# First units' PV held in SBUF, idle identity products early, later softmax sums by head and turned by DMA, and ranks of the plan found by a search

## The chip, the cores and the metric

One core of one Trainium2 chip. The metric is the device time of one execution in microseconds (us), median of several runs. The profile's "span" (first to last instruction) is 1.5 to 2 us shorter. TensorE, VectorE (DVE), ScalarE (ACT), GpSimd (POOL) and the sync engine (SP) run their own instruction streams, each strictly in the order in which the program was emitted; they meet at semaphores. SP here does nothing but issue DMAs.

## The reference, cut to what matters

```python
# q, k, v: 4 batches x 8 heads x 768 positions x 64, float32
scores = (q @ k.T) / 8                     # per batch and head
# heads 0, 2, 6 ("retrieval"): causal; the other five: causal and (first 4 keys or the last 64 keys)
a = exp(scores - max) / (sum + 1e-9)
attn = a @ v                               # -> x: 3072 tokens x 512
h = x @ w_in                               # 512 x 2048
g = h / (1 + exp(-beta * h))
out = g @ w_out                            # 2048 x 512, float32
```

## The kernel before

The work is cut into eight units of 384 queries (`n` = 2·batch + half). A unit's attention makes transposed q and k, scores, exp (no maximum is subtracted), masks, the sums of each softmax row, their reciprocals spread over 64 rows per head (`R`), `PV`, and `xT = PV * R`. Then come 16 up-projection steps (4 products of 384 columns each; ScalarE takes a tanh, VectorE finishes the gate) and 48 down-projection products of 512 columns. Units 0 and 1 start the kernel; the attention of every later unit is laid between the projections of the units before it.

Nobody writes that order down. Every operation is added to a plan with a rank (`key`), an engine, a cost in us, what it needs and gives, and the buffers that it takes and drops. The plan simulates all engines and a DMA bus, takes at each step the operation that can start first (lowest rank on a tie), and the program is then emitted in the simulated order.

```python
    def run(self):
        # ... choose the operation (t, e, o) that can start earliest, lowest rank first ...
            if dma:
                bus = max(bus, t + 0.5) + dma
                end = bus + 1.9            # when the transfer is taken to have landed
        # ...
        return [(f, e) for _, _, f, e in sorted(order, key=lambda x: x[:2])]
```

Once emitted, the order is fixed. If a step takes longer on the chip than the plan thought, everything behind it on its engine waits.

The reciprocals go two ways. Units 0 to 3 (`RD = 4`) split them into two bf16 parts and spread them with four products; units 4 to 7 write them to DRAM and read them back with broadcast. Units 0 to 3 (`TD = 4`) transpose q and k on TensorE, the others by DMA.

```python
    def sums(x):          # 128-column products; columns of queries j*128.. land on rows 32*j + head
        # ... pe.matmul(sm[32*j:32*j+32, 0:128], l, e, ...): 35 of them (even units) or 63 (odd)

    def recips_d(x):                                   # VectorE, straight from PSUM
        x.rec = rp.tile([96, 128], F32, name="rec")
        dve.reciprocal(x.rec, x.sm[0:96, 0:128])

    def spread_w(x):                                   # three DMAs to DRAM
        x.rd = dp.tile([8, TU, 128], F32, name="rd")
        for j in range(TU):
            sp.dma_start(out=x.rd[:, j, :], in_=x.rec[32 * j:32 * j + 8, :])
    # spread_r: two DMAs read rd with broadcast into R (128 x 4 x 384)

    # in the plan, units n >= RD:
            add(key["S"] + 0.1, "dve", 1.0, lambda: recips_d(x), needs=[("sum", n)], gives=[("rec", n)], ...)
            add(key["S"] + 0.2, "sp", 1.4, lambda: spread_w(x), needs=[("rec", n)], gives=[("rd", n)], dma=0.1, ...)
            add(key["S"] + 0.3, "sp", 0.9, lambda: spread_r(x), needs=[("rd", n)], gives=[...R...], dma=4.0, ...)
```

The softmax here doesn't subtract the row's maximum and nothing guards it: scores larger than these inputs give would overflow.

Of the kernel before, what the change touches and what calls it, by code (L numbers as in the profile page):

```python
# [24 lines left out]
TD = 4  # L25
RD = 4
# [23 lines left out]
class _Plan:  # L50
# [16 lines left out]
    def run(self):  # L67
# [11 lines left out]
        while any(left.values()):  # L79
# [39 lines left out]
            now[e] = end  # L119
# [16 lines left out]
            order.append((t, i, f, e))  # L136
            self.log.append((t, i, t + cost, e, key, gives))
        return [(f, e) for _, _, f, e in sorted(order, key=lambda x: x[:2])]
# [3 lines left out]
def kernel(  # L142
# [23 lines left out]
    def tpool(name, bufs, space=None):  # L166
# [4 lines left out]
        q2f=5, k2f=5, vf=3, wf=3, c=4, vb=2, vs=2, xT=2, gT=2, t=2, osb=3, R=1, rec=1, hl=1, VK=2,  # L171
# [56 lines left out]
    def const_ident():  # L228
        pool.memset(warm, 0.0)
        pool.memset(identf, 1.0)  # L230
        aff(identf, 1, -1, 0, 128)
        aff(identf, -1, 1, 0, 128)
        act.activation(out=warm, in_=warm, func=AF.Exp)
        dve.tensor_copy(out=ident, in_=identf)
# [127 lines left out]
    def sink_rows(b):  # L362

        t = bank((2 * b, "k"))
        pe.matmul(t[0:96, :], sink_sel, v_b[b][:, 0, :, :].rearrange("p h d -> p (h d)"), start=True, stop=True)
        held["sinks"] = t
# [32 lines left out]
    def load_beta():  # L399
        held["beta"] = rp.tile([96, 128], F32, name="rec")[0:FO]  # L400
        act.dma_start(out=held["beta"], in_=moe_beta.rearrange("(fo fi) -> fo fi", fi=128))
# [11 lines left out]

    def transposes(x, pi):
        t = ps.tile([128, 2, 512], BF16, name=f"b{plan.where['b', (x.n, 'T', pi)]}")
        x.ps[pi] = t[:, :, 0:NQ].rearrange("p a (t n) -> p a t n", t=TU)
        c = x.ld.pop((pi, "c"))
        for i in range(2):
            for t in range(TU):
                pe.transpose(x.ps[pi][:, i, t, :], c[:, i, t * 128:(t + 1) * 128], ident)  # L420

    def qk_copy(x, pi, eng, i0=0, n=2):
        dst = x.QK[:, i0:i0 + n, pi, x.u * NQ:(x.u + 1) * NQ].rearrange("d a (p t) -> d a p t", t=TU)
        cast(eng, dst, x.ps[pi][:, i0:i0 + n].rearrange("d a t p -> d a p t"))
# [33 lines left out]
    def scores(x, pi, ri):  # L458
# [6 lines left out]
        ps = banks((x.n, pi, ri))  # L465
        halves = rounds[ri]
# [78 lines left out]
    def sums(x):  # L545
        sm = bank((x.n, "s"))
        byj = [[] for _ in range(TU)]
# [17 lines left out]

    def recips_d(x):
        x.rec = rp.tile([96, 128], F32, name="rec")
        dve.reciprocal(x.rec, x.sm[0:96, 0:128])

    def spread_w(x):  # L570
        x.rd = dp.tile([8, TU, 128], F32, name="rd")
        for j in range(TU):
            sp.dma_start(out=x.rd[:, j, :], in_=x.rec[32 * j:32 * j + 8, :])
# [21 lines left out]
    def spread(x, t):  # L595
        if t == 0:
            x.R = rp.tile([128, NP, NQ], F32, name="R", bufs=RINGS["R"])
# [5 lines left out]
    def spread_copy(x, t, eng):  # L603
        cast(eng, x.R[:, t, :], x.ps.pop(("R", t))[:, 0:NQ])

    def pv(x, g):
        vb = v_b[x.b]
        o = banks((x.n, "v", g))
        ops = [[], []]
# [78 lines left out]
    def attention(n, key, early):  # L688
        x = units[n]
        b, u = x.b, x.u  # L690
        gate = ([("begun", "o", NS // 2 - 1)] if b else []) + ([("h", n - 2, 0)] if n > 3 else [])

        for pi in range(NP if n < TD else 0):
            for nm in ("q2", "k2"):
                e = "act" if n == 0 and nm == "k2" else "sp"
                add(key["lq"] + 0.01 * pi, e, 0.47, lambda pi=pi, nm=nm, e=e: load_qk(x, pi, nm, ENG[e]), dma=0.64, needs=gate,
                    gives=[("f", n, pi, nm)], take=[(nm + "f", (n, pi), 1)])
                e = [("pool", "dve"), ("pool", "act")][n] if early else ("pool",)
                add(key["T"][pi] - 2 + (0.001 if nm == "k2" else 0), e, [{"dve": 0.3, "pool": 0.47, "act": 0.41}[i] for i in e],
# [3 lines left out]
                    take=[("c", (n, pi), 1)] if nm == "q2" else [], drop=[(nm + "f", (n, pi))])  # L703
        if n >= TD:
            for i in range(2):
                add(key["lq"] + 0.1 * i, "sp", 3.0, lambda i=i: load_block(x, i), dma=3.9, needs=gate,
                    gives=[("f", n, i)], take=[("wf", (n, "b", i), TU)])
                for j in range(TU):
                    add(key["T"][0] - 2 + 0.5 * j + 0.1 * i, "pool", 0.7, lambda i=i, j=j: cast_block(x, i, j, pool),
                        needs=[("f", n, i)] + ([("c", n, 0, j)] if i else []), gives=[("c", n, i, j)],  # L710
                        take=[("c", (n, j), 1)] if i == 0 else [], drop=[("wf", (n, "b", i))])
            for j in range(TU):
                add(key["T"][0] + 0.5 * j, "sp", 1.25, lambda j=j: turn_block(x, j), dma=0.7,
                    needs=[("c", n, 0, j), ("c", n, 1, j)] + [("sc", n - 4 + v, pi) for pi in range(NP) for v in range(2 - u) if n >= 4],
                    gives=[("QKb", n, j)], drop=[("c", (n, j))])
            add(key["T"][0] + 1.5, "pool", 0.02, lambda: None, needs=[("QKb", n, j) for j in range(TU)],
                gives=[("QK", n, pi, i) for pi in range(NP) for i in range(2)])
        for j in range(TU):
# [6 lines left out]
            add(key["cv"] + 0.5 * j, "pool", 0.58, lambda j=j: cast_v(x, j, pool),  # L725
                needs=[("vf", n, j)] + ([("v", n - u, 0)] if (u, j) != (0, 0) else []),
                gives=[("v", n, j)], drop=[("wf" if b else "vf", (n, 0 if b else j))], take=[("vb", b, 5)] if (u, j) == (0, 0) else [])
        add(key["cv"] + 2, ("dve", "pool") if n else ("pool",), (1.2, 3.0), lambda e: shift_v(x, ENG[e]), port=True,
            needs=[("v", n, j) for j in range(TU)] + ([("v", n - 1, TU - 1)] if u else []), gives=[("vs", n)], take=[("vs", n, 2)])
        if not u:  # L730
            add(key["cv"] + 3, "pe", 0.23, lambda: sink_rows(b), needs=[("v", n, 0), ("const", "sink")], gives=[("VKp", b)],
                take=[("b", (n, "k"), 1)], drop=[("vb", b)])
            add(key["cv"] + 3.1, "dve", 0.6, lambda: sink_copy(b), needs=[("VKp", b)], gives=[("VK", b)],
                take=[("VK", b, 4)], drop=[("b", (n, "k"))])
# [4 lines left out]
        for pi in range(NP if n < TD else 0):  # L739
            k0 = key["T"][pi]  # L740
            wait = [("sc", n - 4 + j, pi) for j in range(2 - u) if n >= 4]
            add(k0, "pe", 0.34 if early else 0.2, lambda pi=pi: transposes(x, pi), needs=[("c", n, pi, "q2"), ("c", n, pi, "k2"), ("const", "ident")],
                gives=[("T", n, pi)], take=[("b", (n, "T", pi), 2 if early else 1)], drop=[("c", (n, pi))])
            if early:
                for i in range(2):
                    add(k0 + 0.1, ("act", "dve"), (0.37, 0.465), lambda e, pi=pi, i=i: qk_copy(x, pi, ENG[e], i, 1),
                        needs=[("T", n, pi)] + wait, gives=[("QK", n, pi, i)], drop=[("b", (n, "T", pi))])
            else:
                add(k0 + 0.1, ("act", "dve"), (0.7, 0.87), lambda e, pi=pi: qk_copy(x, pi, ENG[e]),
                    needs=[("T", n, pi)] + wait, gives=[("QK", n, pi, 0), ("QK", n, pi, 1)], drop=[("b", (n, "T", pi))])  # L750
        for pi in range(1, NP):
            if not u:
                k0 = key["T"][pi]
                add(k0 + 0.2, ("pool", "dve"), (0.35, 0.3), lambda e, pi=pi: ks_copy(x, pi, ENG[e]), port=True,
# [5 lines left out]
        for bi, bu in enumerate(bursts):  # L760
            k0 = key["B"][bi] if not early else key["T"][bu[0][0]] + 0.5 + 0.2 * bu[0][1]
# [18 lines left out]
            for j, (pi, ri) in enumerate(bu):  # L780
                half = rounds_of(pi, u)[ri][1] is None
                add(k0 + 0.1 + 0.02 * j, "act", 0.38 if half else 0.7, lambda pi=pi, ri=ri: exps(x, pi, ri),
                    needs=[("S", n, pi, ri)], gives=[("E", n, pi, ri)], drop=[("sp", (n, pi, ri))])
                c = mask_cost(pi, ri, u)
                if c:
                    add(k0 + 0.2 + 0.02 * j, "dve", c, lambda pi=pi, ri=ri: masks(x, pi, ri, dve), port=True,
# [3 lines left out]
        add(key["S"], "pe", [0.85, 1.35][u], lambda: sums(x), needs=M + [("const", "esel"), ("const", "sink")], gives=[("sum", n)],  # L790
            take=[("b", (n, "s"), 1)], drop=[(f"es{pi}_{u}", n) for pi in range(NP)], mode="sum")
        if n < RD:
            add(key["S"] + 0.1, "dve", 0.88, lambda: recips(x), needs=[("sum", n)], gives=[("rec", n)])
            add(key["S"] + 0.2, "dve", 1.3, lambda: split(x), needs=[("rec", n), ("const", "sel"), ("const", "zero")], gives=[("hl", n)],
                take=[("hl", n, NP)], drop=[("b", (n, "s"))])
            for t in range(NP):
                add(key["S"] + 0.3 + 0.01 * t, "pe", 0.18, lambda t=t: spread(x, t),
                    needs=[("hl", n)] + ([("sb", n, 0)] if t else []), gives=[("sb", n, t)],
                    take=[("b", (n, "R", t), 1)] + ([("R", n, 2)] if t == 0 else []), drop=[("hl", n)])
                add(key["S"] + 0.4, ("act", "dve"), (0.37, 0.465), lambda e, t=t: spread_copy(x, t, ENG[e]),  # L800
                    needs=[("sb", n, t)], gives=[("R", n, t)], drop=[("b", (n, "R", t))])
        else:
            add(key["S"] + 0.1, "dve", 1.0, lambda: recips_d(x), needs=[("sum", n)], gives=[("rec", n)],
                take=[("rec", n, 1)], drop=[("b", (n, "s"))])
            add(key["S"] + 0.2, "sp", 1.4, lambda: spread_w(x), needs=[("rec", n)], gives=[("rd", n)], dma=0.1, drop=[("rec", n)])
            add(key["S"] + 0.3, "sp", 0.9, lambda: spread_r(x), needs=[("rd", n)], gives=[("R", n, t) for t in range(NP)], dma=4.0,
                take=[("R", n, 2)])
        for g in range(2):
            drop = [(f"es{pi}_{u}", n) for pi in [(0, 1, 3), (2, 3)][g]] + [("vb", b), ("vs", n), ("VK", b)]
            add(key["PV"][g], "pe", [[0.5, 0.67], [1.05, 1.2]][u][g], lambda g=g: pv(x, g),  # L810
                needs=M + vready + [("rec", n) if n < RD else ("R", n, 0)], gives=[("o", n, g)], take=[("sp", (n, "v", g), 1)], drop=drop, mode="pv")
            add(key["PV"][g] + 0.1, "dve", 0.87, lambda g=g: norm(x, g),
# [34 lines left out]
    for n in range(N):  # L847
        u = n % 2
        if n == 0:
            attention(n, dict(lq=-100, lv=-99.5, cv=-97.5, T=[-98, -97, -96, -95], S=-94, PV=[-93.9, -93.8]), True)  # L850
        elif n == 1:
            attention(n, dict(lq=-99.4, lv=-99.05, cv=-90, T=[-90, -89, -88, -87], S=-80, PV=[-79.9, -79.8]), True)
        else:
            base = 16 * (n - 1)
            key = dict(lq=base - 34, lv=base - 32, cv=base - 20, T=[base - t for t in (25.5, 24.5, 23.5, 22.5)],
                       B=[base - t for t in ([18, 16, 14], [20, 18, 16, 14, 12, 11])[u]], S=base - 9.5,
                       PV=[base - 4.5, base - 3.5])
            attention(n, key, None)
    add(-99.995, "act", 0.3, load_beta, dma=0.1, gives=[("beta_r",)], take=[("rec", "beta", 1)])
    add(-91, "pe", 0.2, lambda: held.update(t=turn_beta()), needs=[("beta_r",), ("const", "ident")], gives=[("beta_p",)],  # L860
        take=[("b", "beta", 1)], drop=[("rec", "beta")])
# [59 lines left out]
```

## Time and profile before

| | before |
|---|---|
| time, median (range) | 250.34 us (250.06 to 250.45) |
| span of the profiled run | 248.3 us |
| TensorE busy | 228.4 us, 92% |
| first up-projection product starts | 28.16 us |
| last product ends | 244.24 us |

The page of the kernel before: span, busy time per engine, busy tenths of TensorE and of the DMA engines in 40 slices, and the chain that ended last. (PEld is TensorE loading weights; SPq, DVEq and the like are the instruction queue of an engine.)

```profile
span 248.3 us, 5643 instructions
PE 228.4 (92%) x2217; PEld 126.9 (51%) x2245; DVE 151.9 (61%) x319; ACT 144.0 (58%) x246; POOL 71.1 (29%) x158
PE   1649799999999999999999999999999999999993
DMA  6999979999913994079896959996760116111012
PE 85%; DVE 4%; ACT 4%; DMA 3%; issue 2%; ACTq 0%
```

TensorE bounds it: the digits are 9 from the fifth slice on, and 85% of the chain lies on it. The timeline of the kernel before, TensorE only (start, length, engine, line, what; in brackets the idle time before it and what ended it):

```profile
5.19 0.84 PE L44 MATMUL b<-ident,c 128*128 128x128 bf16 x6
...
28.16 0.82 PE L44 MATMUL b<-xT,w_in 128*128 128x384 bf16 x4
...
144.09 0.24 PE L44 MATMUL b<-es,esel_k 96*32 96x128 bf16 x3
144.15 1.46 PE L44 MATMUL b<-es,esel 128*32 128x128 bf16 x60
145.77 0.59 PE L44 MATMUL b<-w_out,gT 128*128 128x512 bf16 x2 [0.16 <-issue]
...
239.76 4.48 PE L44 MATMUL b<-w_out,gT 128*128 128x512 bf16 x19
```

`b<-xT,w_in` is the up-projection, `b<-w_out,gT` the down-projection, `b<-es,esel` the sums. Between 28.16 and 244.24 us the holes of TensorE add up to 0.6 us, besides 12 gaps of 0.16 us with the releaser "issue". Those are probably no holes: such a group shows two down-projection products where its neighbours show three (the last but one line), and this trace holds only 356 of the 384 down-projection products, so records are missing. Time can be won in two ways: a shorter head, or less work on TensorE after it.

### The profile page before, as it was taken

What the parts mean: (1) busy time and instruction counts of PE and PEld (TensorE: products, weight loads), DVE (VectorE), ACT (ScalarE), POOL (GpSimd) and SP (SyncE); (2) the same over time, 40 slices, a digit from 0 to 9 for tenths busy, and PEclk for the clock granted to TensorE, in tenths of its full rate; (3) what the DMA queues carried; (4) which work ended last, traced back from release to release, by engine and by line L of the source; (5) the groups of instructions that cost most, each with busy time, mean ns of one, the idle gap of its engine ahead of it and who ended that gap; (6) DMA issues with size and microseconds to landing.
All of it is one profiled execution on the core that took longest, in us unless ns stands there. A gap on an engine that the chain in (4) does not pass through costs nothing.

```text
span 248.3 us, 5643 instructions
## 1 busy us (share of the span) xinstructions
PE 228.4 (92%) x2217; PEld 126.9 (51%) x2245; DVE 151.9 (61%) x319; ACT 144.0 (58%) x246; POOL 71.1 (29%) x158
## 2 busy tenths in 40 slices
PE   1649799999999999999999999999999999999993
PEld 1416347565564555555546555555545555555441
DVE  6685689888673868566445856667555754554300
ACT  2656994887655955583573945285575834345410
POOL 6373375698330641016200730074000000000000
PEclk9999999999999999999999999999999999999999
DMA  6999979999913994079896959996760116111012
GB/s 204 267 261 279 211 208 343 351 312 211 283 48 99 221 213 107 3 157 221 177 207 147 219 111 196 206 231 133 141 172 29 46 26 150 42 45 42 29 56 84
DMA packets 81530, 40.27 MB, mean 162 GB/s; under 512 B 63984, under 2 KB 74336, under 8 KB 81504
## 3 DMA queue, kind: packets, MB, share of 16 engines
q1 hardware_dynamic: 80384, 39.12, 68.4%
q10 hardware_dynamic: 1120, 0.79, 1.1%
q8 instruction: 17, 0.28, 0.5%
q14 instruction: 9, 0.07, 0.1%
HBM read 30.42 MB, written 6.34 MB: 148 GB/s over the span
## 4 chain that ended last, share of the span: by engine, by line
PE 85%; DVE 4%; ACT 4%; DMA 3%; issue 2%; ACTq 0%
PE b L44 72%; PE sp L44 13%; DMA k2f<-in_k_dram 3%; ACT es L44 2%; DVE es L44 2%; DVE QK L44 1%; ACT t L44 1%; ACT c L44 0%; ACT R L44 0%; DVE vs L44 0%; DVE gT L44 0%; DVE xT L44 0%; ACT osb L44 0%; DVE KS L44 0%; ACT QK L44 0%
## 5 line engine op out<-in xcount | busy, mean ns | idle before, releaser
L44 ACT ACTIVATE t<-b,beta_h 128x384 f32<-128x384 f32 x128 | 72.8, 585 | 51.5 <-PE b L44 46.4
L44 PE MATMUL b<-xT,w_in 128*128 128x384 bf16 x512 | 98.5, 326 | 0.3
L44 DVE SCALAR_TENSOR_TENSOR gT<-t,b 128x384 bf16<-128x384 f32 x128 | 68.8, 552 | 45.0 <-ACT t L44 44.3
L44 PE MATMUL b<-w_out,gT 128*128 128x512 bf16 x356 | 93.8, 379 | 2.6 <-issue 1.9
L44 PEld LDWEIGHTS <-w_in 128*128 128x128 bf16 x512 | 48.5, 98 | 41.1 <-issue 2.1
L44 ACT ACTIVATE es<-sp 128x768 bf16<-128x768 f32 (+1 forms) x68 | 50.9, 794 | 22.9 <-PE sp L44 22.3
L44 PEld LDWEIGHTS <-gT 128*128 128x128 bf16 x384 | 35.5, 98 | 35.0 <-issue 1.6
L44 POOL CAST c<-wf 128x256 bf16<-128x256 f32 x48 | 20.1, 452 | 61.7 <-DMA wf<-in_q_dram 57.4
L44 PE MATMUL sp<-QK 64*64 64x128 bf16 (+4 forms) x420 | 19.8, 256 | 3.6 <-DVE QK L44 1.6
L44 DVE TENSOR_TENSOR es<-es,mask_c 128x256 bf16<-128x256 bf16 (+2 forms) x32 | 10.6, 345 | 14.3 <-ACT es L44 13.7
L44 PEld LDWEIGHTS <-QK 64*64 64x64 bf16 (+1 forms) x420 | 10.4, 109 | 16.2 <-issue 10.3
L44 DVE TENSOR_TENSOR es<-es,mask_s 128x768 bf16<-128x768 bf16 (+1 forms) x24 | 15.0, 634 | 3.8 <-ACT es L44 3.1
L44 DVE TENSOR_TENSOR xT<-sp,R 128x768 bf16<-128x768 f32 x16 | 15.0, 954 | 2.0 <-PE sp L44 1.4
L44 PE MATMUL sp<-es,vb 128*64 128x64 bf16 (+3 forms) x228 | 16.1, 244 | 0.0
L44 ACT ACTIVATE osb<-b 128x512 f32<-128x512 f32 x15 | 8.9, 595 | 12.1 <-PE b L44 11.9
L44 POOL CAST vb<-wf 128x512 bf16<-128x512 f32 x18 | 11.0, 618 | 9.5 <-DMA wf<-in_v_dram 8.9
L44 POOL CAST w_in<-wf 128x512 bf16<-128x512 f32 x16 | 9.6, 640 | 13.4 <-DMA wf<-in_moe_w_in_dram 13.4
L44 ACT COPY QK<-b 128x384 bf16<-128x384 bf16 (+1 forms) x15 | 8.5, 590 | 8.2 <-PE b L44 7.8
L44 PEld LDWEIGHTS <-vb 128*64 128x64 bf16 x228 | 12.1, 113 | 1.4
L44 PE MATMUL b<-ident,c 128*128 128x128 bf16 x96 | 10.2, 253 | 2.4 <-ACT c L44 1.3
L44 PE MATMUL sp<-es,vs 128*64 128x64 bf16 x120 | 11.0, 197 | 0.0
L44 PE MATMUL b<-es,esel 128*32 128x128 bf16 x372 | 10.7, 227 | 0.0
(68 smaller groups left out, 144.7 us busy)
## 6 DMA issues: line engine op xcount, KB each, us to landing
out_dram<-osb SPq DMA_DIRECT2D x24, 256.0 KB, 2.9
wf<-in_v_dram SPq DMA_DIRECT2D x18, 256.0 KB, 5.4
wf<-in_moe_w_out_dram SPq DMA_DIRECT2D x4, 1024.0 KB
q2f<-in_q_dram SPq DMA_DIRECT2D x16, 192.0 KB, 4.9
wf<-in_moe_w_in_dram SPq DMA_DIRECT2D x4, 768.0 KB, 6.3
wf<-in_q_dram SPq DMA_DIRECT2D x12, 256.0 KB, 4.1
wf<-in_k_dram SPq DMA_DIRECT2D x12, 256.0 KB, 5.1
R<-rd SPq DMA_DIRECT2D x8, 384.0 KB, 6.0
```

Source lines behind the costliest of these rows:

```text
L44: ins = f(*a, **k)
```

## The change

Its intent: take work off TensorE, and start the dense stretch earlier.

- **Held PV.** Units 0 and 1 no longer wait with PV for reciprocals: PV is copied to SBUF and multiplied when the spread reciprocals are there.
- **Idle identity products ("fills").** Where the plan sees TensorE idle in the attention of units 0 and 1, it multiplies identity matrices to keep the clock up.
- **Sums by head, turned by DMA** for units 2 to 7 (`RD` from 4 to 2): the sums come in four quarters of 384 columns, one group of heads each (18 or 24 products instead of 35 or 63). They stand as eight rows of 384, too long for a fast reciprocal, so ACT or DVE copies them to SBUF and DMAs turn them into 96 rows of 32. Four DMAs in even units, six in odd ones. The reciprocals then go to DRAM in one DMA instead of three.
- **`TD` from 4 to 3**: unit 3's transposes go to DMA.
- **Ranks found by a search** over the plan replace the formulas; every operation of every unit has its own.

The diff, cut to its core:

```diff
-TD = 4
-RD = 4
+TD = 3
+RD = 2
+QUARTERS = [[[1, 0], [2, 3], [4, 5], [6, 7]], [[0], [2], [6], [1, 3, 4, 5, 7]]]
+KEYS = {0: dict(lq=[-165.82, ...], ...), ...}          # some 400 searched ranks
...
+    def fill(dst):
+        for _ in range(int(held["gap"] / 0.13)):        # gap: idle time before this step in the plan
+            if dst.dtype == BF16: pe.transpose(dst, ident, ident)
+            else: pe.matmul(dst, ident, ident, start=True, stop=True)
...
+    def sums_copy(x, eng):
+        x.sc = rp.tile([128, NQ], F32, name="sc")
+        cast(eng, x.sc, x.sm[:, 0:NQ])
+    def sums_turn(x):
+        x.rec = rp.tile([8 * CR, 32], F32, name="rec")
+        for g, heads in enumerate(QUARTERS[x.u]):
+            at = sorted(XH.index(h) for h in heads)
+            while at:                                    # one DMA for each run of neighbouring heads
+                n = 1
+                while n < len(at) and at[n] == at[0] + n:
+                    n += 1
+                sp.dma_start(out=x.rec[at[0] * CR:(at[0] + n) * CR, :],
+                             in_=x.sc[32 * g + at[0]:32 * g + at[0] + n, :].rearrange("p (c n) -> p c n", n=32))
+                at = at[n:]
     def recips_d(x):
-        x.rec = rp.tile([96, 128], F32, name="rec")
-        dve.reciprocal(x.rec, x.sm[0:96, 0:128])
+        dve.reciprocal(x.rec, x.rec)
...
+            add(key["R"], ("act", "dve"), (0.37, 0.465), lambda e: sums_copy(x, ENG[e]), needs=[("sum", n)], ...)
+            add(key["R"] + 0.1, "sp", [1.2, 2.1][u], lambda: sums_turn(x), needs=[("sum_s", n)], dma=0.1, ...)
+            add(key["R"] + 0.2, "dve", 0.35, lambda: recips_d(x), needs=[("sum_t", n)], ...)
```

## The prediction

> What bounds the kernel now. TensorE: 228.4 of 248.3 us busy (busy table), and the chain of waits lies 85% on it. The timeline shows two regions. From the first up-projection product at 28.16 us to the last product at 244.25 (216 us) TensorE is dense; the table of windows leaves some 4 us idle. Before it, TensorE waits on a chain (last k half landed 9.14; casts, copies, scores, exp, masks; sums 18.9; reciprocal, split, spread, norm until 27.85) and runs at half pace: six 128-column identity products take 0.84 us at 5.19, later 0.50. Warm, the head's products are about 8 us (estimate), so 20 us are loss. The tail after 244.25 stays.
>
> Dense region after the change (estimates from the timeline):
> - Sums, units 2 to 7: now 35 and 63 matmuls of 128 columns, 0.96 and 1.52 us, often with a 0.16 "issue" gap. New: 18 and 24 matmuls, longest quarter 1408 and 2304 columns, about 0.65 and 1.05 us. Saves 2.6 us over six units.
> - Spread of units 2 and 3 by DMA: 8 matmuls of 0.16 us, 1.3 us.
> - Unit 3's transposes by DMA: four groups of 0.34 to 0.43 us, 1.5 us.
> Together 5.4 us. The longer road of the reciprocals (copy, turn, reciprocal, write, read; the read alone 6.0 us) should hide, as units 4 to 7 hide a similar one.
>
> The head. Identity products in planned gaps should warm the clock earlier. The Trainium skill ("TensorE: Matmul & The Clock Gate", Part 1) says the array starts at half rate and about 3.4 us of sustained work releases it; the trace agrees in pace (0.12 against about 0.06 us start to start). That shortens sums (1.71 to about 0.9 us), scores and PV. PV no longer follows the reciprocal: held copies (0.8 us) run during reciprocal and split (2.3 us); after the spread stand four DVE products (about 0.55 each) instead of copies (1.0) and two norms (1.9), 0.7 us saved. Unit 0's shift may leave POOL, where it takes 3.66 us at 12.87 while two masks take 3.10 us on DVE instead of about 1.3; the Trainium skill ("SBUF — State Buffer", SBUF: two separate sides) describes such an exclusive port lock, and the doubled mask time agrees. Searched ranks should close holes. I expect the first up-projection at 24 us, 4 earlier; the chain's durations hardly allow less than 20.
>
> What pulls back: DMA share is near 1 until 60 us, and weights must come earlier too (last w_in casts end at 42). The search used a model, so I take off 1 us for holes and late weights.
>
> Sum: 5.4 + 4 - 1 = 8.5 or so; 250.3 becomes 241.8 us, range 237 to 246.5. Faster 0.84, same 0.14, slower 0.02.
>
> Signs: first up-projection at 23 to 25 us; last product near 236; between them about 211 us against 216; sums about 0.65 and 1.05 us; no transposes by product after unit 2; more TensorE instructions in the head; DVE products of 384 columns in place of the R copies; masks at 12 to 16 us below 0.9 each.
>
> What would make it wrong: PV of units 2 and 3 stalled by late reciprocals; fills that overrun their gaps and delay real work; late weights; or a much better head, down to 20 us.

## The result, and the profile after

| | before | after |
|---|---|---|
| time, median (range) | 250.39 us (250.06 to 250.53) | 256.91 us (256.75 to 258.54) |
| ratio of fast runs | | 1.028 (1.023 to 1.032) |
| first up-projection product | 28.16 us | 25.66 us |
| last product ends | 244.24 us | 251.34 us |
| TensorE holes after the first up-projection product (without "issue") | 0.6 us | 13.5 us |

All runs quoted are fast. Ratios are the mean time of one kernel's fast runs over that of the other's in the same rounds, so they are not quite the ratio of the medians.

The change made the kernel slower by 2.8%, while I had forecast 3.4% faster. The head did get shorter, by 2.5 us. The dense stretch, from which 5 us of work was taken, got longer by 9.6 us. The page of the changed kernel:

```profile
span 255.0 us, 5440 instructions
PE 230.1 (90%) x2103; PEld 125.5 (49%) x2103; DVE 139.3 (55%) x308; ACT 143.9 (56%) x239; POOL 74.8 (29%) x166
PE   3887999899989999699779959999999899999994
DMA  7999999999776985999989929997216033101122
PE 50%; DMA 21%; SPq 14%; POOL 6%; DVE 4%; issue 2%; ACT 2%; DVEq 0%; POOLq 0%; ACTq 0%
```

There are holes (the digits 6, 7 and 5) in the middle of TensorE's row, and the chain that ended last now lies only 50% on TensorE: 21% on transfers (3% before) and 14% on SP's queue, which did not appear before. The timeline of the changed kernel, TensorE only, at the places shown before:

```profile
25.66 0.98 PE L97 MATMUL b<-xT,w_in 128*128 128x384 bf16 x5
...
144.00 1.00 PE L97 MATMUL b<-es,esel 128*32 128x384 bf16 x23
144.83 0.33 PE L97 MATMUL b<-es,esel_k 96*32 96x384 bf16 x1
145.09 2.12 PE L97 MATMUL b<-w_out,gT 128*128 128x512 bf16 x9
...
247.72 3.62 PE L97 MATMUL b<-w_out,gT 128*128 128x512 bf16 x16
```

The odd unit's sums now take 1.09 us (144.00 to 145.09) where they took 1.52 (144.09 to 145.61). That part works as intended. The waits of the changed kernel (who waited for what: us in total, times, longest) show where the rest went:

```profile
DVE rec L97 <- DMA rec<-sc: 20.3, 6, 4.7
...
PE b L97 <- DVE gT L97: 6.0, 4, 2.7
PE sp L97 <- DMA QK<-c: 5.5, 4, 2.4
```

VectorE stands 20.3 us behind six short reciprocals whose turned sums have not landed. Two kinds of TensorE holes follow, 6.0 and 5.5 us: products waiting for the gate step (`gT`) that VectorE does late, and scores waiting for q and k that were transposed late by DMA. Unit 5's case, all engines of the changed kernel:

```profile
145.20 0.48 ACT L97 COPY sc<-b 128x384 f32<-128x384 f32 x1 [2.51 <-PE b L97]
145.70 4.79 SPq L97 DMA_DIRECT2D rec<-sc  x6
145.97 0.96 DVE L97 TENSOR_TENSOR xT<-sp,R 128x768 bf16<-128x768 f32 x1
...
151.67 0.35 DVE L97 RECIPROCAL rec<-rec 96x32 f32<-96x32 f32 x1 [4.74 <-DMA rec<-sc]
151.94 0.95 DVE L97 SCALAR_TENSOR_TENSOR gT<-t,b 128x384 bf16<-128x384 f32 x2
...
152.48 0.32 PE L97 MATMUL b<-xT,w_in 128*128 128x384 bf16 x1 [2.68 <-DVE gT L97]
```

SP needs 4.79 us to issue six small DMAs, which the plan had at 2.1. The reciprocal runs 6.0 us after the first issue instead of 2.5 (by the plan's formula, 0.5 + 0.1 + 1.9). VectorE had been given that reciprocal as its next step, so it stood still for 4.74 us; the gate steps behind it were late, and TensorE ran dry for 2.68 us. Over the six units the time from first issue to reciprocal is 4.1 to 4.6 us (even) and 5.9 to 6.0 (odd).

The hole costs more than its length. The table of windows of the changed kernel just after it (busy us of PE, PEld, DVE, ACT and POOL; then the granted TensorE clock):

```profile
150.00:154.00 4.00, 1.52 (x9) 0.89 (x9) 1.77 (x4) 1.48 (x3) 0.00 (x0) 0.95 0.42 76
154.00:158.00 4.00, 4.00 (x17) 2.00 (x16) 2.21 (x4) 2.19 (x5) 0.00 (x0) 0.62 1.33 156
158.00:162.00 4.00, 4.00 (x27) 2.39 (x25) 3.30 (x6) 3.58 (x7) 1.03 (x2) 1.00 1.23 218
```

The clock falls to 0.95 and 0.62 for two windows: (0.05 + 0.38) × 4 us = 1.7 us more are lost. (The clock record of the packed trace has it as one stretch of 3.41 us at half clock.)

### The profile page after: what moved, and what is told of

It reads as the page before. It is cut to its first block, busy times and chain, and to the rows that moved or that the text cites. A ratio compares the mean times of both kernels' runs of the same rounds, so it can differ in the third digit from the quotient of the medians.

```text
span 255.0 us, 5440 instructions
## 1 busy us (share of the span) xinstructions
PE 230.1 (90%) x2103; PEld 125.5 (49%) x2103; DVE 139.3 (55%) x308; ACT 143.9 (56%) x239; POOL 74.8 (29%) x166
## 4 chain that ended last, share of the span: by engine, by line
PE 50%; DMA 21%; SPq 14%; POOL 6%; DVE 4%; issue 2%; ACT 2%; DVEq 0%; POOLq 0%; ACTq 0%
PE b L97 44%; SPq L97 14%; PE sp L97 6%; DMA wf<-in_moe_w_in_dram 6%; DMA wf<-in_v_dram 4%; DMA q2f<-in_q_dram 4%; DMA rec<-sc 3%; DMA wf<-in_moe_w_out_dram 3%; POOL w_out L97 2%; POOL vb L97 1%; DMA QK<-c 1%; DVE gT L97 1%; POOL w_in L97 1%; POOL vs L97 1%; ACT t L97 1%
## 5 line engine op out<-in xcount | busy, mean ns | idle before, releaser
L97 PE MATMUL b<-xT,w_in 128*128 128x384 bf16 x512 | 92.3, 330 | 5.0 <-DVE gT L97 4.4
L97 PE MATMUL b<-w_out,gT 128*128 128x512 bf16 x384 | 91.5, 380 | 1.6 <-DVE gT L97 1.6
L97 POOL CAST c<-wf 128x256 bf16<-128x256 f32 x60 | 23.0, 426 | 48.2 <-DMA wf<-in_q_dram 31.4
L97 ACT ACTIVATE osb<-b 128x512 f32<-128x512 f32 x18 | 10.6, 596 | 37.2 <-PE b L97 35.6
L97 PE MATMUL sp<-QK 64*64 64x128 bf16 (+6 forms) x420 | 19.8, 245 | 8.3 <-DMA QK<-c 5.5
L97 DVE TENSOR_TENSOR es<-es,mask_s 128x768 bf16<-128x768 bf16 (+1 forms) x24 | 13.3, 566 | 12.8 <-ACT es L97 12.4
L97 DVE TENSOR_TENSOR xT<-sp,R 128x768 bf16<-128x768 f32 x12 | 11.1, 954 | 12.5 <-PE sp L97 9.5
L97 DVE RECIPROCAL rec<-rec 96x32 f32<-96x32 f32 x6 | 2.1, 349 | 20.3 <-DMA rec<-sc 20.3
L97 POOL CAST w_out<-wf 128x512 bf16<-128x512 f32 x16 | 10.0, 676 | 2.7 <-DMA wf<-in_moe_w_out_dram 2.6
L97 PEld LDWEIGHTS <-vs 128*64 128x64 bf16 x120 | 9.2, 111 | 1.6 <-issue 1.4
```

Source lines behind the costliest of these rows:

```text
L97: ins = f(*a, **k)
```

## The experiments

Theory 1: the road of the reciprocals is the cause, because its turn takes longer than the order was made for. Rival 2: SP is overloaded by something else of the change (unit 3's transposes and loads) and delivers q and k late. Rival 3: fills or ranks. Twelve kernels ran. "Order kept" means that the plan was run with the figures of the changed kernel, and only what is emitted at one place differs. All runs were fast but four, which are named below and left out of the ratios.

### Reciprocals later in VectorE's order

```diff
+LATE = (2.5, 4.0)     # us in plan time, even and odd units: reciprocal, write and read are emitted that much later
+        order = [(t + max([LATE[g[1] % 2] for g in x[5] if g[0] in ("rec", "rd", "R") and g[1] >= RD] or [0.0]), i, f, e, gap)
+                 for (t, i, f, e, gap), x in zip(order, self.log)]
```

> The changed kernel with the same order on every engine, except that the six short reciprocals of units 2 to 7 and the DMA issues after them (write, read) are emitted 2.5 us (even units) or 4.0 us (odd units) later in plan time. Theory 1 (VectorE runs in order and stands still behind a reciprocal whose turned sums are not there yet; the plan reckoned 2.5 us from first turn issue to reciprocal, the trace shows 3.3 to 6.0): VectorE's wait on the turn falls from 20.3 us to below 8, the TensorE holes released by gT products (1.56 and 2.68 us and two small ones) go, time 249 to 252 us. Rival 2 (the loss comes from the sync queue, which issues the DMA transposes of q and k too late): the holes before scores (1.26, 2.35, 1.40, 0.47 us) stay and time stays at 255 us or more. Rival 3 (the head: fills): no change.

Measured: 257.46 us (256.81 to 258.43), ratio to before 1.027: no gain, a miss. The mechanism did what it should and the time did not follow. The waits of this run:

```profile
DVE rec L98 <- DMA rec<-sc: 5.9, 2, 4.9
...
PE sp L98 <- DMA QK<-c: 4.9, 3, 2.5
...
PE sp L98 <- DVE xT L98: 3.0, 2, 2.5
PE b L98 <- DVE xT L98: 2.4, 2, 2.0
```

VectorE's wait fell from 20.3 to 5.9 us and the holes behind `gT` to 0.4 us. In their place came 5.4 us of holes behind `xT`, the norm, which needs the read at the road's end. The holes behind late transposes stayed (4.9 us). This run's trace also has two half-clock stretches where the changed kernel's has one, another 1.7 us. Moving the waiting step moves the wait; what has to go, it seems, is the length of the road and SP's time in it, and the runs below test that.

### The road of before in the changed kernel

```diff
 def sums_copy(x, eng):      # now at its place in VectorE's order: the reciprocal straight from PSUM
+    x.rec = rp.tile([96, 128], F32, name="rec"); dve.reciprocal(x.rec, x.sm[0:96, 0:128])
 def sums_turn(x), recips_d(x):
+    pass
 # sums(x) in place of sums_d(x), three write DMAs as before; order kept
```

> The changed kernel with its order kept, but units 2 to 7 take their sums, reciprocal and three write DMAs in the form of the kernel before (the reciprocal straight from PSUM at the place of the sums copy; no turn by DMA). TensorE has 2.6 us more of sums. Theory 1: no VectorE wait on a DMA before a reciprocal, gT holes gone; with the 30 turn issues of 0.73 us (22 us of the sync queue) gone as well, rival 2's holes shrink too: 247 to 251 us. If instead the searched ranks, the fills or unit 3's DMA transposes are the cause, time stays at 255 us or more.

Measured: 248.88 us (247.93 to 249.97), ratio to before 0.993 (0.988 to 0.997). With everything else of the change in place (ranks, fills, held PV, `TD = 3`, `RD = 2`), going back to the old road alone wins 8 us, although TensorE again does the longer sums. This clears rival 3 of most of the loss. The holes behind late transposes fell to 2.4 us, so most of rival 2's sign belonged to the road too.

### The road alone in the kernel before

```diff
 # kernel before, ranks and RD = 4 kept: units 4 to 7 get sums_d, sums_copy, sums_turn, the short reciprocal and one write
```

> The kernel before with only one part of the change: units 4 to 7 take sums by head, the copy, the turn by DMA and the short reciprocal; ranks, head and units 0 to 3 as before. TensorE loses about 1.8 us of sums. Theory 1: VectorE waits 2 to 5 us per unit on the turn, part of it comes through to TensorE: 250 to 256 us. If the road were harmless: 248.5 us.

Measured: 259.71 us (258.80 to 259.98), ratio 1.035. The part alone costs 9 us, more than I had expected, in four units only, with no searched rank, no fill and no moved transposes. TensorE's waits in this run name the same two kinds of holes:

```profile
PE sp L46 <- DMA QK<-c: 5.4, 3, 2.9
...
PE b L46 <- DVE gT L46: 3.0, 2, 2.2
```

### No fills

```diff
-        for _ in range(int(held["gap"] / 0.13)):
+        for _ in range(0):
```

> The changed kernel without any of its idle identity products, order kept. In its trace 40 of them run from 4.17 to 7.85 us, while the first cast inputs are ready at 5.34 us, so they hold the first transposes up by about 2.3 us, but TensorE is warm after them. Without them the first transposes start near 5.4 us at half pace. If the hold-up is as large as the warm clock's gain, the first up-projection stays at 25 to 27 us and time within 1.5 us of the changed kernel; if fills help on balance, time rises by 1.5 us or more; if they hurt, it falls.

Measured: 252.94 us (252.31 to 255.90), about 4 us below the changed kernel. That is more than the head explains. The timeline of this run has the first up-projection 0.45 us earlier than with fills (25.66), though its early products ran at half pace:

```profile
7.16 0.50 PE L97 MATMUL b<-ident,c 128*128 128x128 bf16 x3 [1.12 <-DVE c L97]
...
25.21 0.98 PE L97 MATMUL b<-xT,w_in 128*128 128x384 bf16 x5
```

With fills such a group of three takes 0.33 us (at 7.68 us). So the fills do warm the clock, and the head gains nothing by it here; they also hold the first transposes up by 2.6 us (7.68 against 5.09). The rest of the 4 us was not settled. The mean clock does not explain it: it was 0.998 to 1.000 in three of these four runs against 0.980 to 0.993 in three of the four runs of the changed kernel, but the changed kernel's fourth run, at 1.000, took 257.07 us and was no faster than the others. The one profiled run (255.9 us, clock 0.993) is close to the changed kernel's 256.8. It holds a wait of 1.99 us for the cast of a part of w_in and then a half-clock stretch (1.7 us), together about what it took more than the other three (252.3 to 253.0 us); those were not profiled, so this is not shown.

### The turn in one issue, with wrong data

```diff
-        pool.memset(esel, 0.0)
+        pool.memset(esel, 0.0078125)      # every row of the sums finite
 def sums_turn(x):                         # one DMA of eight rows (wrong rows) in place of four or six; order kept
+    x.rec = rp.tile([8 * CR, 32], F32, name="rec")
+    sp.dma_start(out=x.rec, in_=x.sc[0:8, :].rearrange("p (c n) -> p c n", n=32))
```

> Wrong result on purpose. The changed kernel, order kept, every step of the road kept (copy, turn by DMA, short reciprocal, write, read), but the turn is one DMA of eight rows in place of four (even units) or six (odd units); the stationary zeros of the sums become a small constant so that every row read is finite. It takes away only the number of issues, about 0.73 us each. Theory 1 in its sharper form (the turn's issues are the cause: the plan reckoned 1.2 and 2.1 us, the trace shows 3.4 and 4.8, and both VectorE behind the reciprocal and the q/k transposes behind the turn on the sync queue come late by the difference): first issue to reciprocal falls to 2.5 to 3.3 us, VectorE's wait on the turn from 20.3 us to below 13, TensorE holes from 14.8 us to below 9, time 246 to 250 us. If instead the long chain of three transfers as such is the cause, time stays above 253 us.

Measured: 244.50 us (243.93 to 244.77), ratio to before 0.978 (0.976 to 0.981); the result is wrong, as meant. Every step of the road is still there and as many bytes are turned; only the number of issues went from 30 to 6. That is worth 12 us against the changed kernel, more than I had expected. VectorE's wait on the turn fell to 6.7 us. The tile view of `rec` (duration of an issue in ns: lowest, median, highest) gives for the changed kernel

```profile
L97 SPq DMA_DIRECT2D rec<-sc x30: 628/727/877, 63.2 to 201.7; - x30
```

and for the run with one issue

```profile
L97 SPq DMA_DIRECT2D rec<-sc x6: 747/766/1084, 64.4 to 186.4; - x6
```

An issue of this form takes 0.73 us for 12 to 36 pieces of 128 bytes and 0.77 us for 96 of them: it is paid by the DMA, not by its size. The write that follows moves the same 96 pieces to DRAM, and its issue takes 0.37 us (median), so the pieces alone do not make it dear; whether the target in SBUF or the way the source rows are cut does was not tested. SP spends 30 × 0.73 = 22 us on the turns in one kernel and 4.6 us in the other. This settles theory 1 in its sharp form (a correct run below rules out that the wrong data did it), and rival 2's holes go with it (0.5 us left). One figure I had wrong: from the first issue to the reciprocal it took 2.2 to 2.4 us in four units (said: 2.5 to 3.3) and 4.0 us in the first; in one, VectorE came later without having waited. How the 12 us divide between VectorE's wait and the late transposes, which both went, is known only from the holes (6.0 and 4.9 us).

### Reciprocal of the long rows, no turn

```diff
 def sums_copy(x, eng):
+    x.rec = rp.tile([128, NQ], F32, name="rec"); dve.reciprocal(x.rec, x.sm[:, 0:NQ])
 # no turn; four or six DMAs write the rows to DRAM; order kept
```

> The changed kernel, order kept, sums by head kept, but no copy and no turn: VectorE takes the reciprocal of all 128x384 sums straight from PSUM (by the measured 0.95 us for 128 columns about 2.9 us), and four or six DMAs write its rows. TensorE keeps the 2.6 us that sums by head save against the run with the old road. If that saving reaches the end and 2.9 us of VectorE in one piece do no harm: 2 us below the old road's 248.9, so 246 to 248. If VectorE's block costs as much as the saving: 248 to 251. If the row writes hold the sync queue up as the turn did: 252 or more.

Measured: 253.96 us (252.71 to 257.00, the last a slow run), ratio 1.014. The time lies where I had put it for a held-up SP, but the reason is another. The tile view of `rec` shows 0.25 us for each of the 30 row writes, a third of a turn's issue. It is VectorE that holds the others up:

```profile
L97 SPq DMA_DIRECT2D rd<-rec x30: 235/250/875, 69.8 to 200.0; - x30
L97 DVE RECIPROCAL rec<-b x6: 2546/2558/2558, 61.4 to 195.7; 128x384 f32<-128x384 f32 x6
...
  PE b L97: 4.0, 4
```

One reciprocal of 384 columns blocks VectorE for 2.56 us, and products waited 4.0 us for it in four places (last line: who waited for it); norms behind it cost 2.2 us more, and a half-clock stretch another 1.7 us. The kernel before pays 0.95 us for 128 columns on 96 rows.

### Honest figures in the plan, same ranks

```diff
-                end = bus + 1.9
+                end = max(bus, t + cost) + 1.9
-            add(key["R"] + 0.1, "sp", [1.2, 2.1][u], lambda: sums_turn(x), ...)
+            add(key["R"] + 0.1, "sp", [2.9, 4.8][u], lambda: sums_turn(x), ...)
```

> The changed kernel with the same ranks, and only the plan's figures for the turn set to what the trace shows (2.9 and 4.8 us of the sync queue, landing 1.9 us after the last issue); the plan then orders all engines anew. If the loss is only that the order was made for a turn that is too fast, the new order hides it: 247 to 251 us. If the turn takes more of the sync queue than there is to spare, or if the searched ranks fit only the order they were searched with: 253 us or more.

Measured: 262.33 us (261.02 to 263.49), ratio 1.049, the slowest of all. With true figures the plan makes a new order, and with the same ranks it is a worse one. TensorE's waits in this run:

```profile
PE sp L97 <- DVE xT L97: 7.7, 3, 5.5
...
PE b L97 <- DVE xT L97: 3.9, 3, 3.3
```

11.6 us of holes stand behind norms, up to 5.5 us in one piece, and 10.2 us at half clock cost 5.1 us more. The wait on the turn is down to 5.3 us. The searched ranks belong to the figures that they were searched with. Whether a new search on true figures would have hidden the turn was not tried.

### Only unit 3's transposes moved

```diff
 # kernel before
-TD = 4
+TD = 3
```

> The kernel before with only unit 3's transposes moved from TensorE to DMA. My prediction reckoned 1.5 us off TensorE where it is dense: 248.5 to 249.5 us. Rival: unit 3's loads through three shared buffers and its transposes on the sync queue come late and eat it: 250 us or more.

Measured: 248.96 us (248.21 to 249.32) against 250.21, ratio 0.995 (0.993 to 0.998). This part is worth 1.2 us of the 1.5 that I had reckoned.

### A correct turn in one issue

The sums repeat each head's row four times within its quarter (row 32·quarter + 8·copy + head). If odd units group their heads as even ones do, the eight heads stand on rows 0, 17, 34, ... 119, so one DMA with a step of 17 rows can read them.

```diff
-QUARTERS = [[[1, 0], [2, 3], [4, 5], [6, 7]], [[0], [2], [6], [1, 3, 4, 5, 7]]]
+QUARTERS = [[[1, 0], [2, 3], [4, 5], [6, 7]]] * 2
 def sums_turn(x):                         # order kept
     x.rec = rp.tile([8 * CR, 32], F32, name="rec")
+    sp.dma_start(out=x.rec, in_=x.sc[0:120:17, :].rearrange("p (c n) -> p c n", n=32))
```

> A correct form of the one-issue turn, in the changed kernel, order kept. Odd units group the heads in quarters as even units do ((1,0), (2,3), (4,5), (6,7)), so that with the sums repeated four times in each quarter the eight heads stand on rows 0, 17, 34, ... 119, and one DMA with a step of 17 rows turns them. Odd sums take 2688 columns in the longest quarter instead of 2304, 0.16 us more each, 0.5 us in all. Theory 1 (number of issues): 244.5 plus 0.5, so 244 to 246 us, VectorE's wait on the turn 5 to 9 us. If the wrong data of the earlier one-issue run, not its single issue, made it fast: 250 us or more.

Measured: correct, 245.14 us (243.96 to 247.38), ratio to before 0.980 (0.977 to 0.984). It beats both kernels; whether it is 2% faster than the kernel before is open, as the interval ends at 0.984. Its page, as above:

```profile
span 242.2 us, 5390 instructions
PE 226.4 (93%) x2088; PEld 126.5 (52%) x2112; DVE 138.9 (57%) x308; ACT 144.1 (59%) x239; POOL 74.6 (31%) x166
PE   3887899989999999999999999999999999999993
```

The row of TensorE is full again. The chain that ended last, not shown, still lies only 59% on TensorE, with 12% on SP's queue and 10% on transfers, so its shares alone were no measure of the loss; the holes are. Its waits, for two of the three that had made the loss (the third, products behind `gT`, is not in the list):

```profile
DVE rec L97 <- DMA rec<-sc: 6.4, 3, 4.1
...
PE sp L97 <- DMA QK<-c: 0.6, 2, 0.3
```

The timeline gives the ends of the dense stretch, 26.27 us and 235.77 + 2.75 = 238.52 us:

```profile
26.27 0.98 PE L97 MATMUL b<-xT,w_in 128*128 128x384 bf16 x5
...
235.77 2.75 PE L97 MATMUL b<-w_out,gT 128*128 128x512 bf16 x12
```

The books nearly close. From the first up-projection product to the last product it takes 13.4 us less than the changed kernel (225.7 to 212.3 us). All holes of the changed kernel there were 13.5 us, of which 2.0 remain (those behind `gT` and behind q and k: 6.0 + 5.5 us, of which 0.6 remain); its slow-clock stretch cost 1.7 us; the odd quarters give 0.5 us back. That is 12.6 of the 13.4 us. The last product ends only 12.8 us earlier (251.34 to 238.52), because the stretch starts 0.6 us later: in this run the 40 fills took 4.45 us instead of 3.68, as the clock rose later (at 8.65 us instead of 6.86).

### The same without fills, and with a shorter first fill

```diff
 # no fills:            for _ in range(0):
 # shorter first fill:  for _ in range(int((held["gap"] - (4.1 if held["gap"] > 4.1 else 0)) / 0.13)):
```

> The one-issue kernel without any idle identity products. Theory: TensorE isn't what the head waits for (the first up-projection came 0.5 us earlier without them, although TensorE ran at half pace until 17.7 us), so time is within 1 us of the one-issue kernel, rather below. If the warm clock helped: 1.5 us or more above it.

> The one-issue kernel with fills, but the first of them reckoned from the time at which the identity is there (4.1 us) and not from zero: some 9 products instead of 40. The first transposes should start near 5.4 us instead of 7.7. If the overrun delayed the head: 1 to 2 us below the one-issue kernel. If the head is bound by ScalarE's exps, casts and transfers: within 0.7 us.

Measured: 245.05 us (243.70 to 247.77, the last a slow run), ratio 0.979, without fills; 247.86 us (244.90 to 249.34, the two highest slow), ratio 0.984, with the short one. The first up-projection starts at 25.1 and 25.0 us against 26.3. Fills are worth nothing here: the starts are even 1.2 us earlier without them (of which 0.6 us is how slowly the fills happened to run in the one-issue kernel's profiled run), and the time is the same. With the short fill the first transposes start at 5.07 us and the products run at the fast pace from 11.4 us, without fills only from 18.0; yet the first up-projections start within 0.14 us of each other. So from 11.4 us on the pace of TensorE is not what the head waits for. The short fill was expected to help or to do nothing; its median is 2.7 us higher. Its runs fall into two groups, 244.9 and 245.4 us at a mean clock of 1.000 and 247.3 to 249.3 us at 0.993 (the two slow ones among them). Its profiled run is of the second group, and its table of windows shows the stretch:

```profile
26.00:30.00 4.00, 2.67 (x32) 1.48 (x30) 2.27 (x5) 3.71 (x7) 2.29 (x4) 1.00 0.96 174
30.00:34.00 4.00, 2.89 (x12) 1.41 (x12) 1.27 (x3) 1.16 (x2) 3.78 (x7) 0.73 0.95 249
34.00:38.00 4.00, 4.00 (x76) 2.82 (x75) 2.59 (x5) 1.42 (x3) 2.18 (x4) 0.84 1.02 334
```

TensorE has a hole of 1.99 us there, waiting for the cast of a part of w_in, and then runs two windows at 0.73 and 0.84. An earlier start of the projections came up against weights that were not there.

### The mended road alone in the kernel before

```diff
 # as "the road alone in the kernel before", with the one-issue turn and its quarters
```

> The kernel before with the new road of the reciprocals alone (units 4 to 7), as in the earlier run of 259.7 us, but with the turn in one issue. Theory 1: the loss of 9 us goes, and the sums' saving of about 1.5 us shows in part: 248 to 251 us. If the road's extra transfer as such hurts in this order: 253 us or more.

Measured: 251.15 us (249.66 to 251.49) against 250.05, ratio 1.002 (0.999 to 1.006). The 9 us are gone, and nothing is won: what the shorter sums save is spent elsewhere (1.7 us of holes behind late transposes are in its trace). Three of its four runs had a mean clock of 0.993, and the profiled one of them has a half-clock stretch, 1.7 us; the run at 1.000 took 249.66 us.

## Why the prediction was wrong, point by point

- **The step that failed:** "The longer road of the reciprocals (copy, turn, reciprocal, write, read; the read alone 6.0 us) should hide, as units 4 to 7 hide a similar one." I gave it 0 us. It cost about 12 us: 256.91 against 245.14 and 244.50 with the turn in one issue. I looked at how long the road is and asked whether PV would stall. I did not cost its issues on SP, thirty of 0.73 us, nor did I ask what stands behind the waiting steps in the fixed orders of VectorE and SP. I also had no duration for this form of DMA in the trace of before; the row writes there take 0.29 us (median), and the turn's issue takes 2.5 times that. The list of what would make me wrong named "PV of units 2 and 3 stalled by late reciprocals". In the changed kernel it was the gate steps and the next units' scores that stalled.
- **5.4 us off TensorE in the dense stretch: right, once the turn is out of the way.** From first up-projection to last product I said 211 us against 216; the one-issue kernel has 238.52 - 26.27 = 212.3, with 0.5 us of it added by its odd quarters. In the changed kernel it is 225.7. The sums take 0.72 and 1.09 us (said: 0.65 and 1.05), so over three pairs they save 2.0 us and not 2.6: I had counted the missing records' gaps in. Unit 3's transposes are worth 1.2 us alone (said: 1.5).
- **First up-projection at 24 us: too early.** It came at 25.66 us, 2.5 us sooner instead of 4.
- **The warm clock in the head: mechanism right, worth wrong.** The pace doubled, as predicted and as the Trainium skill ("TensorE: Matmul & The Clock Gate", Part 1) has it: three identity products in 0.33 instead of 0.50 us. The start of the projections did not move by it; without fills it came 0.45 us sooner in the changed kernel and 1.2 us in the one-issue kernel (0.6 us of the latter is the slower pace of its fills). The granted clock in the profiles does not show this: it reads 1.00 at half pace too, because its record begins with the first change, at 22.85 us in the kernel before and at 6.86 in the changed one. One reason is in the trace: 40 fills run from 4.17 to 7.68 us, while without fills the first transposes start at 5.09 us; the gap was counted from zero, and the identity is ready only at 4.1. What else bounds the head (ScalarE's exps, which run 5.16 us in one piece from 11.37 us, or transfers) was not tested.
- **The port lock:** the two masks fell from 3.10 us together to 0.54 and 0.96 us (said: below 0.9 each), with unit 0's shift on VectorE. This agrees with the lock of the Trainium skill ("SBUF — State Buffer", SBUF: two separate sides), but its share of the head was not measured alone.
- **1 us for holes and late weights:** late weights did show (1.99 us) as soon as the head got shorter.

## What to carry to other kernels

On an in-order engine, count every issue of a new transfer at a duration measured for that same form (here 0.73 us from SBUF to SBUF against 0.25 for a row write to DRAM), and multiply by the number of DMAs before you look at bytes. Then look at what stands behind the waiting step in each engine's order: a 0.35 us reciprocal made 20 us of waits. A schedule searched on a cost model is only as good as its figures, and the same priorities on corrected figures can be worse than either; if a step is dearer than the model says, make the step cheaper or search again. (Here only the first was tried; issuing some of the turns from another engine was not.)

## What the Trainium skill lacked or had wrong

- "DMA: Bandwidth & Descriptors", Issuing engines are not separate DMA queues, says that the sequencer's time to initiate a DMA is "usually small relative to the DMA itself". In these runs a small SBUF-to-SBUF DMA kept SP for 0.73 us (0.77 with 96 pieces), of the 1.8 to 2.0 us from the start of a unit's last issue to the reciprocal that waited for it; thirty of them cost 12 us of kernel time. I found no figure on the page by which a reader could tell this form (0.73 us) from a row write to DRAM (0.25 us).
- "TensorE: Matmul & The Clock Gate", Why this matters for your kernels, advises no idle gaps above about 3 us. Here holes of 2.68 us and 1.99 us were followed by windows at a clock of 0.62 and 0.73, while other holes of 2.4 and 2.7 us were not, in the same kernel or in the same place of another run. In the kernel before with the mended road a half-clock stretch followed a hole of only 1.23 us (and one of 0.38 us before it). Each of these three stretches lasted 3.41 us and so cost 1.7 us.
- The same page, Part 4, says that transposes do not bring the full clock. In the changed kernel the first 40 fills are all transposes by the kernel's code (the profile lists them as MATMUL, so their mode on the chip is not shown), nothing else ran on TensorE before or between them, and after 26 of them, at 6.9 us, their distance from start to start fell from 0.107 to 0.056 us. Right after them three products took 0.33 us, the fast pace (0.50 us for such a group without the fills).
- "VectorE: DVE Perf Modes", First, the fixed hardware budget, tells that a reciprocal repeats its divide, but I found no time by size there. The runs show 0.35 us for 32 columns (96 rows), 0.95 us for 128 (96 rows), 2.56 us for 384 (128 rows, from PSUM).
